# A convolution feeding a gated FFN on one core: four steps of sixteen clip on ScalarE, the convolution's taps are spread over other steps, and the low parts' products come last

## The chip, the cores and the metric

The kernel runs on one core of a Trainium2 chip. The metric is device time in microseconds (us) of one execution. A core has a matmul engine (TensorE, PE in the profile; its weight loads are PEld), two engines for elementwise work that can read the matmul's accumulators in PSUM (VectorE, DVE; ScalarE, ACT), a third that works in SBUF alone (GpSimd, POOL), and SyncE (SP), whose queue issues the DMA transfers here. Each engine takes its instructions strictly in program order and waits where one of them needs something that another engine has not finished.

## The reference

The input x has 8 sequences of 4096 tokens with 192 channels. First comes a causal convolution over 7 tokens whose weights are a softmax per head (8 heads of 24 channels), then a feed-forward layer on the 32768 resulting tokens, 192 to 2048 to 192, with a clipped quadratic between its two matrices:

```python
w = softmax(weight, axis=-1)                       # [8, 7]
out[b, s, h, :] = sum_k w[h, k] * x_pad[b, s + k, h, :]
h = out.reshape(32768, 192) @ w_in                 # [32768, 2048]
g = where(h >= 1, h, where(h <= -1, 0, (h + 1)**2 / 4))
return g @ w_out                                   # [32768, 192]
```

The quadratic can be had in three operations in two ways. The kernel before writes it as max(h, ((c + 1) / 2) squared) with c = h clipped to -1..1. The other form, used by it for the first seven steps only, is max(h, min(1, relu((h + 1) / 2) squared)).

## The kernel before, in words

The tokens are worked in 64 blocks of 512 (the index s, or superblock). Hidden units are taken 256 at a time, so a block takes 8 steps and the program has 512 steps q. Two blocks share one round of convolution work, so everything repeats after 16 steps; i = q mod 16 is the place of a step in this round, and a round has blocks A (i = 0 to 7) and B (i = 8 to 15).

Precision near that of fp32 comes from splitting each operand of a product into a high part, rounded to a shorter format, and a low part, the remainder: `hi` and `lo` (`rh`, `rl` and their swapped copies for the 64 channels above 128, "the rest"), `gh` and `gl` for the hidden values, and weights in two parts. Three partial products are summed for each product.

In step q the program issues, engine by engine:

- PE: `mm1(q)` (line 422), 18 matmuls that form the hidden values `h` of step q in PSUM (two buffers, so `mm1(q)` needs the reads of `h` of step q-2 done), then `mm2(q-2)` (line 462), 20 matmuls that add the product of `gh` and `gl` of step q-2 with the second matrix into four accumulators, `accm` (two) and `accr` (two). In `mm2` eight matmuls on `gh` go into `accm`, then four on `gl` into `accm`, four on `gh` into `accr` and four on `gl` into `accr`. The accumulators have a single buffer: the first `mm2` of the next block (in steps with i = 2 and i = 10) must find them copied out.
- DVE: `act_clip(q)` (line 473, the clip, reading `h` from PSUM), `act_lo(q-1)` (line 497, `gl` = `g` minus `gh`, two operands in SBUF), `act_max(q)` (line 484, reading `h` and `g`), then transposes for the convolution (line 147) and for the output (`osb`, line 534) where such are due.
- ACT: `act_hi(q-1)` (line 491, the cast to `gh`), `act_square(q)` (line 479), in steps with i = 1 and i = 9 the evacuation `evac` of the four accumulators (line 509, four copies to tiles `t`), then what the convolution's plan puts into this step.
- POOL: sums of the evacuated halves (lines 511 and 522), the convolution's adds (line 230) and the low part `lo` (line 252).

The convolution of the next inputs runs beside this on ACT, POOL and DVE. It has three units per round: A and B are the first 128 channels of the two blocks (B is needed in step 8 of the same round, A and R in step 0 of the next), R is the rest of both. A unit begins with a transpose "T" on DVE into a tile `xT`; tap 0 is a scaled copy into `y` on ACT (line 226), each further tap is a product `p` on ACT (line 219) and an add `y + p` on POOL (line 230); at the end "split" makes the high part on ACT (line 248, or 262 for R), the low part on POOL (line 252; for R on DVE, line 263), and the DMAs that swap the two halves of the partitions (lines 235 and 236). `conv_slot(i, ...)` issues the parts that the tables `PLAN_B`, `PLAN_A`, `PLAN_R` name for place i; it stands behind `act_max` in a step. The order on every engine is that in which the program is written; no scheduler moves anything. `xT` and `y` have two buffers each, `p` three.

Of the kernel before, what the change touches and what calls it, by code (L numbers as in the profile page):

```python
# [13 lines left out]
AF = mybir.ActivationFunctionType  # L14
# [16 lines left out]
def lightconv_then_ffn(ctx: ExitStack, tc: tile.TileContext, x, weight, w_in, w_out, out):  # L31
# [24 lines left out]
    nc = tc.nc  # L56
# [8 lines left out]
    NPAIR = NF // 2  # L65
# [44 lines left out]
    def load_unit(c, u, engs=None):  # L110
        ta, tb = 2 * c * TB, (2 * c + 1) * TB
        if u == "rb":
            return load_raw([tb, tb, tb + TB // 2, tb + TB // 2], [P, P + SQ, P, P + SQ], engs,
                            TB // 2)
        if u == "r":
            return load_raw([ta, ta, tb, tb], [P, P + SQ, P, P + SQ], engs)
        return load_raw([ta if u == "a" else tb] * 4, [0, SQ, 2 * SQ, 3 * SQ], engs)
# [14 lines left out]
    NF32 = 2 * NPAIR  # L132
# [257 lines left out]
    NQ = NSB * NPAIR  # L390
    hs, g32, gs, ghs, gls, accs = {}, {}, {}, {}, {}, {}

    def turns(t):

        return t.rearrange("p (o c) -> p c o", o=2)

    def both(t):
        return t.rearrange("p (c o) -> p c o", o=2)
# [4 lines left out]
    def mm1(q):  # L403

        s, j = divmod(q, NPAIR)

        if q == 0:
            h = hs[q] = [ps_o.tile([P, TB], F32, name=n) for n in ("accr1", "accm0")]
        else:
            h = hs[q] = ps_h.tile([P, 2, TB], F32, name="h")  # L410
            h = [h[:, e, :] for e in range(2)]

        if s == 0:
            mms = [(WI[j], us, [xop[s][u] for u in us]) for us in ("ns", "sn", "rr")]
        else:
            mms = [(W[j][:, part], u + u, [xop[s][u, x]] * 2) for u in "nsr"
                   for part, x in ((0, "hi"), (1, "hi"), (0, "lo"))]
        for n, (w, us, x) in enumerate(mms):
            for e in range(2):
                c0 = COL[us[e]][e]  # L420
                to, of = (both(h[e]), turns(x[e][e])) if in_turns(s) else (h[e], x[e][e])
                nc.tensor.matmul(to, w[HALVES[e], c0:c0 + P], of,  # L422
                                 start=(n == 0), stop=(n == len(mms) - 1))

    def new_accs(s):
        accs[s] = {(a, i): ps_o.tile([P, TB], F32, name=f"acc{a}{i}")
                   for a in "mr" for i in range(2)}

    def mm2_first(q):


        s, j = divmod(q, NPAIR)
        g, w = g32.pop(q), WF[j + LAG]
        if j == 0:
            new_accs(s)
        for e in range(2):
            for b in range(TB // P):
                a, c0 = "mr"[b // 2], b % 2 * D
                for i, half in enumerate(HALVES):
                    nc.tensor.matmul(accs[s][a, i][:, c0:c0 + D], g[half, e, b * P:(b + 1) * P],  # L440
                                     w[half, e, :], start=(j == 0 and e == 0 and b % 2 == 0),
                                     stop=(j == NPAIR - 1 and e == 1 and b % 2 == 1))

    def mm2(q):

        s, j = divmod(q, NPAIR)
        gh, gl = ghs.pop(q), gls.pop(q)
        w, wr, k = W[j + LAG], WR[j + LAG], n_in[j + LAG]
        if j == 0:
            new_accs(s)  # L450
        m0, m1, r0, r1, r = ("m", 0, gh), ("m", 1, gh), ("m", 0, gl), ("r", 0, gh), ("r", 0, gl)
        mms = [(e, m) for ms in ((m0, m1), (r0,), (r1,), (r,)) for e in range(2) for m in ms]
        if q == NQ - 1:
            mms = [(0, m) for m in (r1, m0, m1, r, r0)] + [(1, m) for m in (r1, r, m0, m1, r0)]
        first = {a: min(n for n, (e, m) in enumerate(mms) if m[0] == a) for a in "mr"}
        last = {a: max(n for n, (e, m) in enumerate(mms) if m[0] == a) for a in "mr"}
        for n, (e, (a, part, g)) in enumerate(mms):
            c0 = k + e * P
            for i in range(2):
                st = (w[HALVES[i], part, c0:c0 + P] if a == "m"  # L460
                      else wr[HALVES[i], e].rearrange("p a d -> p (a d)"))
                nc.tensor.matmul(both(accs[s][a, i]), st, turns(g[HALVES[i], e, :]),  # L462
                                 start=(j == 0 and n == first[a]),
                                 stop=(j == NPAIR - 1 and n == last[a]))


    def tiles(q):
        return [slice(0, 1), slice(1, 2)] if q == NQ - 1 else [slice(0, 2)]

    def act_clip(q):  # L470
        g = gs[q] = act.tile([P, 2, TB], F32, name="g", bufs=3)
        for e in tiles(q):
            nc.vector.tensor_scalar(out=g[:, e, :], in0=hs[q][:, e, :], scalar1=-1.0, scalar2=1.0,  # L473
                                    op0=ALU.max, op1=ALU.min)

    def act_square(q):
        g = gs[q]
        for e in tiles(q):
            nc.scalar.activation(g[:, e, :], g[:, e, :], AF.Square, bias=0.5, scale=0.5)  # L479

    def act_max(q):
        h, g = hs.pop(q), gs[q]
        for e in tiles(q):
            nc.vector.tensor_tensor(out=g[:, e, :], in0=h[:, e, :], in1=g[:, e, :], op=ALU.max)  # L484
        if q < NF32:
            g32[q] = gs.pop(q)

    def act_hi(q):
        gh = ghs[q] = act.tile([P, 2, TB], F32R, name="gh", bufs=3)
        for e in tiles(q):  # L490
            nc.scalar.copy(gh[:, e, :], gs[q][:, e, :])  # L491
# [209 lines left out]

    PLAN_B = {0: (0, 1), 2: (2, 3), 3: (4, 5), 4: (6,), 5: "split"}
    PLAN_A = {4: ("T", 0), 5: (1, 2), 6: (3, 4), 7: (5, 6), 8: "split"}
    PLAN_R = {7: ("T",), 8: (0, 1, 2), 10: (3, 4), 11: (5, 6), 13: "split"}


    FIRST_B = {2: 2, 3: 3, 4: 4, 5: 5}
# [4 lines left out]
    def conv_slot(i, b, a, r):  # L714
        early = b.c == 0
        plans = ((None if early else b, PLAN_B), (a, FIRST_A if early else PLAN_A),
                 (r, FIRST_R if early else PLAN_R))
        for u, plan in plans:
# [20 lines left out]
    def parts_hi(q):  # L739
        for n, rest in PARTS.get(q, ()):  # L740
            chunks[n].hi(rest)
# [17 lines left out]
    def most(h, g):  # L759

        nc.vector.scalar_tensor_tensor(out=g, in0=g, scalar=1.0, in1=h, op0=ALU.min, op1=ALU.max)
# [75 lines left out]
    for q in range(NQ + DELAY):  # L837
        s, j = divmod(q, NPAIR)
        c, i = divmod(q, 2 * NPAIR)
        done = q - DELAY  # L840
        if q < NQ and i == 0 and c > 0:
            conv_b = conv_n["b"]
        if q < NQ and i == (0 if c > 0 else 4):
            conv_n = {}
            if c + 1 < NB:
                conv_n = {u: Conv(c + 1, u, load_unit(c + 1, u)) for u in "arb"}


        if q == NPAIR:
            mm2_first(done)  # L850
        if q < NQ:
            mm1(q)
        if done >= 0 and q != NPAIR:
            (mm2 if done >= NF32 else mm2_first)(done)

        if q < 2:
            (step_0, step_1)[q]()
        elif q < NPAIR:
            first_step(q)
        else:  # L860
            if q - 1 in gs:
                act_hi(q - 1)
            if q == NPAIR + 1:
                evac(0)
            if q == 2 * NPAIR - 2:
                pending.extend(late)
            if q < NQ:
                let_go()
                act_clip(q)
                act_square(q)  # L870
            if done % NPAIR == NPAIR - 1 and done >= NPAIR:
                (evac if done < NQ - 1 else evac_last)(done // NPAIR)
            parts_hi(q + 1)
            if q - 1 in gs:
                act_lo(q - 1, nc.vector)
            parts_lo(q, (True,))
            if q < NQ:
                let_go()
                act_max(q)
                parts_lo(q, (False,))  # L880
                conv_slot(i, conv_b, conv_n.get("a"), conv_n.get("r"))

            m, r = (DELAY, DELAY + 1) if s > 1 else (NPAIR - 2, NPAIR - 1)
            if q < NQ and j == m:
                evac_rest(s - 1)
                store(s - 1, "m")
            elif q < NQ and j == r:
                store(s - 1, "r")
        if q < NQ and i == 2 * NPAIR - 1 and conv_n:
            conv_n["b"].transpose()  # L890
        if q == NQ - 4:
            plain = ob.tile([P, TB // SQ, SQ], F32, name="osb").rearrange("p j b -> p (j b)")[:, 0:P]
            diagonal(plain, 0)
# [26 lines left out]
```

## Time and profile before

| what | value |
|---|---|
| median of 3 runs | 2170.52 us (2169.75 to 2170.53) |
| the profiled execution, its own time | 2170.33 us |
| its span, first to last instruction | 2168.6 us |
| granted TensorE clock | 0.999 |
| instructions in the span | 48144 |
| PEld busy | 1875.8 us, 86% |
| DMA traffic | 110.83 MB, mean 51 GB/s |

The profile gives, per engine, the busy time and its share of the span; groups of instructions by line and shape with their count, the busy time and the mean duration; and for each engine what ended the times in which it waited. Matmuls overlap one another, so a PE that is 99% busy may still lose time: what tells is the time from the start of one step's `mm1` to that of the next. A timeline row gives the start, the duration, the engine, the line, and in square brackets the idle time before it with the instruction that ended it.

### The profile page before, as it was taken

Reading aid. Unit: us, or ns where it says so; the run is one execution under the profiler, and the core shown is the slowest. Engines: PE = TensorE matmul, PEld = TensorE weight load, DVE = VectorE, ACT = ScalarE, POOL = GpSimd, SP = SyncE. Lnnn points to the kernel's source line nnn. Section 1 sums busy time; section 2 is a strip of 40 time slices with the busy share of each in tenths; the row PEclk is TensorE's granted clock in tenths of the full one; section 3 lists DMA queues with packets and bytes.
Section 4 is the critical chain, followed back from the end, with each engine's and each line's share of the span. In section 5 each row is a group of like instructions: output and inputs, shape, how many; then the busy total and the mean of one; then the engine's idle time right before and its main releaser. Section 6 shows DMA issues by size and latency. Waiting matters only on the chain.

```text
span 2168.6 us, 48144 instructions
## 1 busy us (share of the span) xinstructions
PE 2153.0 (99%) x19646; PEld 1875.8 (86%) x19646; DVE 2084.0 (96%) x1883; ACT 1684.8 (78%) x2153; POOL 1139.4 (53%) x868
## 2 busy tenths in 40 slices
PE   9999999999999999999999999999999999999999
PEld 6998888888888888888888888888888888998887
DVE  8899999999999999999999999999999999999998
ACT  7778877778777788777887787877878777788775
POOL 1556644566445565555654456644556545565451
PEclk9999999999999999999999999999999999999999
DMA  6222222222222222222122222222222222212211
GB/s 165 51 53 42 46 50 51 53 51 42 51 48 50 55 41 53 51 48 55 37 51 51 51 53 48 44 49 48 53 55 40 53 51 47 56 35 53 51 35 25
DMA packets 439197, 110.83 MB, mean 51 GB/s; under 512 B 407360, under 2 KB 414912, under 8 KB 438976
## 3 DMA queue, kind: packets, MB, share of 16 engines
q1 hardware_dynamic: 438816, 107.65, 25.9%
q8 instruction: 155, 2.54, 0.5%
q14 instruction: 66, 0.54, 0.1%
q10 hardware_dynamic: 160, 0.10, 0.0%
HBM read 32.84 MB, written 25.17 MB: 27 GB/s over the span
## 4 chain that ended last, share of the span: by engine, by line
DVE 27%; PE 24%; ACT 19%; POOL 13%; issue 13%; SPq 3%; DMA 1%; POOLq 0%; DVEq 0%; ACTq 0%
POOL y L230 11%; PE h L422 10%; DVE g L484 9%; DVE g L473 8%; PE accm L462 7%; DVE gl L497 7%; ACT g L479 6%; ACT gh L491 5%; PE accr L462 4%; ACT t L509 4%; DVE osb L534 2%; SPq L95 2%; ACT p L219 2%; POOL lo L252 2%; DMA raw<-in_x_dram 1%
## 5 line engine op out<-in xcount | busy, mean ns | idle before, releaser
L230 POOL TENSOR_TENSOR y<-y,p 128x512 f32<-128x512 f32 x546 | 793.8, 1454 | 751.0 <-DVE g L484 541.5
L497 DVE TENSOR_TENSOR gl<-g,gh 128x1024 fp32r<-128x1024 f32 (+1 forms) x497 | 734.4, 1478 | 51.6 <-ACT gh L491 41.3
L491 ACT CAST gh<-g 128x1024 fp32r<-128x1024 f32 (+1 forms) x497 | 520.4, 1047 | 255.4 <-DVE g L484 244.1
L422 PE MATMUL h<-hi,w 64*128 64x512 f32 x4032 | 701.2, 377 | 0.0
L479 ACT ACTIVATE g<-g 128x1024 f32<-128x1024 f32 (+1 forms) x505 | 535.1, 1060 | 167.3 <-DVE g L473 157.0
L484 DVE TENSOR_TENSOR g<-h,g 128x1024 f32<-128x1024 f32 (+1 forms) x505 | 613.3, 1215 | 8.3 <-ACT g L479 4.4
L473 DVE TENSOR_SCALAR g<-h 128x1024 f32<-128x1024 f32 (+1 forms) x505 | 604.7, 1198 | 11.6 <-PE h L422 10.6
L462 PE MATMUL accm<-gh,w 64*128 64x512 f32 x3968 | 604.2, 378 | 9.3 <-ACT t L509 9.1
L422 PEld LDWEIGHTS h<-hi,w 64*128 64x128 f32 x4032 | 523.7, 186 | 47.9
L422 PE MATMUL h<-lo,w 64*128 64x512 f32 x2016 | 540.5, 376 | 0.0
L462 PEld LDWEIGHTS accm<-gh,w 64*128 64x128 f32 x3968 | 449.4, 186 | 77.0 <-ACT t L509 29.4
L462 PE MATMUL accm<-gl,w 64*128 64x512 f32 x1984 | 379.2, 381 | 0.0
L219 ACT ACTIVATE p<-xT,wk 128x512 f32<-128x512 f32 x562 | 376.2, 714 | 0.0
L462 PE MATMUL accr<-gh,wr 64*128 64x512 f32 x1984 | 373.4, 376 | 0.0
L462 PE MATMUL accr<-gl,wr 64*128 64x512 f32 x1984 | 373.4, 376 | 0.0
L422 PEld LDWEIGHTS h<-lo,w 64*128 64x128 f32 x2016 | 330.2, 186 | 24.6
L422 PE MATMUL h<-rh,w 64*128 64x512 f32 x992 | 293.5, 376 | 0.0
L422 PE MATMUL h<-rhi,w 64*128 64x512 f32 x992 | 293.5, 376 | 0.0
L462 PEld LDWEIGHTS accm<-gl,w 64*128 64x128 f32 x1984 | 250.9, 186 | 33.4 <-DVE gl L497 12.3
L462 PEld LDWEIGHTS accr<-gl,wr 64*128 64x128 f32 x1984 | 257.3, 186 | 24.8 <-DVE gl L497 0.2
L462 PEld LDWEIGHTS accr<-gh,wr 64*128 64x128 f32 x1984 | 257.3, 186 | 24.7 <-ACT gh L491 0.2
L422 PEld LDWEIGHTS h<-rhi,w 64*128 64x128 f32 x992 | 184.5, 186 | 14.9
(141 smaller groups left out, 1867.6 us busy)
## 6 DMA issues: line engine op xcount, KB each, us to landing
out_dram<-osb SPq DMA_DIRECT2D x366, 64.0 KB
raw<-in_x_dram SPq DMA_DIRECT2D x334, 68.0 KB
hi<-hi SPq DMA_DIRECT2D x126, 128.0 KB
lo<-lo SPq DMA_DIRECT2D x126, 128.0 KB
rhi<-rh SPq DMA_DIRECT2D x62, 128.0 KB
rlo<-rl SPq DMA_DIRECT2D x62, 128.0 KB
words<-in_moe_w_in_dram SPq DMA_DIRECT2D x16, 192.0 KB
words<-in_moe_w_out_dram SPq DMA_DIRECT2D x8, 384.0 KB
```

Of the source, the lines that this page charges most:

```text
L95: (engs[i] if engs else nc.sync).dma_start(out=raw[i * SQ:(i + 1) * SQ, lo:n // SQ + 1, :], in_=src.rearrange("(j a) b -> a j b", a=SQ),)
L219: nc.scalar.mul(p, self.xT[:, SH + k:SH + k + TB], wk[:, self.wsel, k:k + 1])
L230: nc.gpsimd.tensor_add(y, y, self.product(k))
L252: eng.tensor_sub(lo, self.y, hi.bitcast(F32))
L422: nc.tensor.matmul(to, w[HALVES[e], c0:c0 + P], of, start=(n == 0), stop=(n == len(mms) - 1))
L462: nc.tensor.matmul(both(accs[s][a, i]), st, turns(g[HALVES[i], e, :]), start=(j == 0 and n == first[a]), stop=(j == NPAIR - 1 and n == las ...
L473: nc.vector.tensor_scalar(out=g[:, e, :], in0=hs[q][:, e, :], scalar1=-1.0, scalar2=1.0, op0=ALU.max, op1=ALU.min)
L479: nc.scalar.activation(g[:, e, :], g[:, e, :], AF.Square, bias=0.5, scale=0.5)
L484: nc.vector.tensor_tensor(out=g[:, e, :], in0=h[:, e, :], in1=g[:, e, :], op=ALU.max)
L491: nc.scalar.copy(gh[:, e, :], gs[q][:, e, :])
L497: eng.tensor_sub(gl[:, e, :], g[:, e, :], gh[:, e, :])
L509: nc.scalar.copy(t[i][:, n], acc[a, i][:, n])
```

## The change

Three things are changed.

1. `by_act(q)` is true where i is 0, 4, 5 or 12, from step 16 to step 509. In such a step ACT forms relu(0.5 h + 0.5) from PSUM (line 479 of the new file) in place of DVE's clip, and squares it in place (line 488); `act_max` becomes `most`, one DVE instruction that takes the minimum with 1 and the maximum with `h` (line 775). The relu is issued at the head of ACT's step, in front of the cast of step q-1. In the other steps nothing changes here; their square is line 491 in the new file, the cast 505, the clip 482, `gl` 511, the maximum 498.
2. `mm2` keeps its eight matmuls on `gh` for `accm`, but then takes `accr`'s four on `gh`, and the eight on `gl` come last.
3. The three plans name other places. B: taps 1 to 6 in steps 2, 3 and 4, two each. A: the transpose stays in step 4, tap 0 moves from step 4 to 5, taps to steps 6, 7 (three of them) and 8, the split from step 8 to 10. R: the transpose moves from step 7 to 4, tap 0 alone stays in step 8, the others go two each to steps 10, 11 and 12; the split stays in step 13.

Counted over the program, DVE issues 124 instructions fewer (the clips; 124 maxima become `most`), ACT 124 more; POOL, PE and SP issue as many as before.

```diff
--- before.py
+++ after.py
@@ -449,7 +449,7 @@
         if j == 0:
             new_accs(s)
         m0, m1, r0, r1, r = ("m", 0, gh), ("m", 1, gh), ("m", 0, gl), ("r", 0, gh), ("r", 0, gl)
-        mms = [(e, m) for ms in ((m0, m1), (r0,), (r1,), (r,)) for e in range(2) for m in ms]
+        mms = [(e, m) for ms in ((m0, m1), (r1,), (r0,), (r,)) for e in range(2) for m in ms]
         if q == NQ - 1:
             mms = [(0, m) for m in (r1, m0, m1, r, r0)] + [(1, m) for m in (r1, r, m0, m1, r0)]
         first = {a: min(n for n, (e, m) in enumerate(mms) if m[0] == a) for a in "mr"}
@@ -467,20 +467,34 @@
     def tiles(q):
         return [slice(0, 1), slice(1, 2)] if q == NQ - 1 else [slice(0, 2)]
 
+    BY_ACT = (0, 4, 5, 12)
+
+    def by_act(q):
+
+        return q % (2 * NPAIR) in BY_ACT and NF32 <= q < NQ - 2
+
     def act_clip(q):
         g = gs[q] = act.tile([P, 2, TB], F32, name="g", bufs=3)
+        if by_act(q):
+            nc.scalar.activation(g, hs[q], AF.Relu, bias=0.5, scale=0.5)
+            return
         for e in tiles(q):
             nc.vector.tensor_scalar(out=g[:, e, :], in0=hs[q][:, e, :], scalar1=-1.0, scalar2=1.0,
                                     op0=ALU.max, op1=ALU.min)
 
     def act_square(q):
         g = gs[q]
+        if by_act(q):
+            nc.scalar.activation(g, g, AF.Square)
+            return
         for e in tiles(q):
             nc.scalar.activation(g[:, e, :], g[:, e, :], AF.Square, bias=0.5, scale=0.5)
 
     def act_max(q):
         h, g = hs.pop(q), gs[q]
-        for e in tiles(q):
+        if by_act(q):
+            most(h, g)
+        for e in () if by_act(q) else tiles(q):
             nc.vector.tensor_tensor(out=g[:, e, :], in0=h[:, e, :], in1=g[:, e, :], op=ALU.max)
         if q < NF32:
             g32[q] = gs.pop(q)
@@ -701,9 +715,9 @@
 
 
 
-    PLAN_B = {0: (0, 1), 2: (2, 3), 3: (4, 5), 4: (6,), 5: "split"}
-    PLAN_A = {4: ("T", 0), 5: (1, 2), 6: (3, 4), 7: (5, 6), 8: "split"}
-    PLAN_R = {7: ("T",), 8: (0, 1, 2), 10: (3, 4), 11: (5, 6), 13: "split"}
+    PLAN_B = {0: (0,), 2: (1, 2), 3: (3, 4), 4: (5, 6), 5: "split"}
+    PLAN_A = {4: ("T",), 5: (0,), 6: (1, 2), 7: (3, 4, 5), 8: (6,), 10: "split"}
+    PLAN_R = {4: ("T",), 8: (0,), 10: (1, 2), 11: (3, 4), 12: (5, 6), 13: "split"}
 
 
     FIRST_B = {2: 2, 3: 3, 4: 4, 5: 5}
@@ -858,6 +872,9 @@
         elif q < NPAIR:
             first_step(q)
         else:
+            ahead = q < NQ and by_act(q)
+            if ahead:
+                act_clip(q)
             if q - 1 in gs:
                 act_hi(q - 1)
             if q == NPAIR + 1:
@@ -866,7 +883,8 @@
                 pending.extend(late)
             if q < NQ:
                 let_go()
-                act_clip(q)
+                if not ahead:
+                    act_clip(q)
                 act_square(q)
             if done % NPAIR == NPAIR - 1 and done >= NPAIR:
                 (evac if done < NQ - 1 else evac_last)(done // NPAIR)
```

How this moves instructions is seen at three places. The first is ACT in steps 4 and 5 of a round (from the cast of step 3 to the last convolution piece of step 5). Before:

```order
L491 CAST gh<-g 128x1024
L479 ACTIVATE g<-g 128x1024
L219 ACTIVATE p<-xT,wk 128x512
L226 ACTIVATE y<-xT,wk 128x512
L491 CAST gh<-g 128x1024
L479 ACTIVATE g<-g 128x1024
L248 CAST hi_14329<-y 128x512
L219 ACTIVATE p<-xT,wk 128x512 x2
```

and with the change, from the relu of step 4:

```order
L479 ACTIVATE g<-h 128x1024
L505 CAST gh<-g 128x1024
L488 ACTIVATE g<-g 128x1024
L219 ACTIVATE p<-xT,wk 128x512 x2
L479 ACTIVATE g<-h 128x1024
L505 CAST gh<-g 128x1024
L488 ACTIVATE g<-g 128x1024
L248 CAST hi_14331<-y 128x512
L226 ACTIVATE y<-xT,wk 128x512
```

A's tap 0 (`y<-xT`), which needs the transpose that DVE issues at the end of step 4, stood ahead of the cast `gh` of step 5 and now stands behind it; a relu that reads `h` stands ahead of each cast.

The second is DVE in the same two steps. Before:

```order
L473 TENSOR_SCALAR g<-h 128x1024
L497 TENSOR_TENSOR gl<-g,gh 128x1024
L484 TENSOR_TENSOR g<-h,g 128x1024
L147 STREAM_TRANSPOSE xT<-raw 128x544
L473 TENSOR_SCALAR g<-h 128x1024
L497 TENSOR_TENSOR gl<-g,gh 128x1024
L484 TENSOR_TENSOR g<-h,g 128x1024
```

and with the change:

```order
L511 TENSOR_TENSOR gl<-g,gh 128x1024
L775 SCALAR_TENSOR_TENSOR g<-g,h 128x1024
L147 STREAM_TRANSPOSE xT<-raw 128x544 x2
L511 TENSOR_TENSOR gl<-g,gh 128x1024
L775 SCALAR_TENSOR_TENSOR g<-g,h 128x1024
```

Both clips are gone, and R's transpose, which came in step 7, stands behind A's.

The third is `mm2` on PE, its last twelve matmuls. Before:

```order
L462 MATMUL accm_5826<-gl,w_96 128x512
L462 MATMUL accm_5827<-gl,w_96 128x512
L462 MATMUL accm_5826<-gl,w_96 128x512
L462 MATMUL accm_5827<-gl,w_96 128x512
L462 MATMUL accr_5828<-gh,wr_104 128x512
L462 MATMUL accr_5829<-gh,wr_104 128x512
L462 MATMUL accr_5828<-gh,wr_104 128x512
L462 MATMUL accr_5829<-gh,wr_104 128x512
```

(four on `gl` for `accr` follow) and with the change:

```order
L462 MATMUL accr_5825<-gh,wr_104 128x512
L462 MATMUL accr_5826<-gh,wr_104 128x512
L462 MATMUL accr_5825<-gh,wr_104 128x512
L462 MATMUL accr_5826<-gh,wr_104 128x512
L462 MATMUL accm_5823<-gl,w_96 128x512
L462 MATMUL accm_5824<-gl,w_96 128x512
L462 MATMUL accm_5823<-gl,w_96 128x512
L462 MATMUL accm_5824<-gl,w_96 128x512
```

The first matmul on `gl` comes four matmuls later than it did, the first into `accr` four earlier.

## The prediction, made before the changed kernel ran

> **What bounds the kernel now.** I read the page's busy times first: PE is busy throughout, and DVE nearly so, hence either may set the pace.
>
> ```profile
> PE 2153.0 (99%) x19646; PEld 1875.8 (86%) x19646; DVE 2084.0 (96%) x1883; ACT 1684.8 (78%) x2153; POOL 1139.4 (53%) x868
> ```
>
> What PE could do at best is in the windows view for `mm1`'s line alone (us, then PE and PEld busy with counts). 18 matmuls are one step. The first window begins where a round begins; the second lies in the last round, in which no new A and R are convolved.
>
> ```profile
> 152.65:2091.20 1938.55, 1049.74 (x8352) 859.39 (x8353) 1.00 0.26 49
> 2091.20:2152.70 61.50, 34.73 (x270) 28.29 (x271) 1.00 0.12 23
> ```
>
> The last round does 270/18 = 15 steps in 61.50 us, 4.100 us each. The long stretch has 8352/18 = 464 steps in 1938.55 us, 4.178 each. At 4.100 they would take 1902.4, so 36.1 us are lost over 29 rounds, 1.25 a round. That is all PE can win there. A matmul's share of a full step is 4.100/38 = 0.108 us.
>
> The waits view for 150 to 2100 us (who waited for whom: us, times, longest) says for what:
>
> ```profile
> DVE gl L497 <- ACT gh L491: 39.6, 106, 0.6
> ...
> PEld accm L462 <- ACT t L509: 29.4, 58, 0.7
> PEld accm L462 <- DVE gl L497: 12.3, 54, 0.3
> PE accm L462 <- ACT t L509: 9.1, 28, 0.3
> ```
>
> PE's line waits for two things alone: the evacuation (58 weight loads, two in each of 29 rounds) and `gl`. One round's timeline shows both, in steps 9 and 10:
>
> ```profile
> 1057.60 2.65 POOL L230 TENSOR_TENSOR y<-y,p 128x512 f32<-128x512 f32 x2
> ...
> 1058.54 0.59 PE L422 MATMUL h<-hi,w 64*128 64x512 f32 x4
> ...
> 1059.20 2.13 DVE L497 TENSOR_TENSOR gl<-g,gh 128x1024 fp32r<-128x1024 f32 x1
> ...
> 1060.48 1.03 PE L462 MATMUL accm<-gh,w 64*128 64x512 f32 x8
> ...
> 1061.26 1.21 DVE L484 TENSOR_TENSOR g<-h,g 128x1024 f32<-128x1024 f32 x1
> ...
> 1061.39 0.70 PE L462 MATMUL accm<-gl,w 64*128 64x512 f32 x4
> ...
> 1062.39 1.21 DVE L473 TENSOR_SCALAR g<-h 128x1024 f32<-128x1024 f32 x1
> 1062.43 3.65 POOL L230 TENSOR_TENSOR y<-y,p 128x512 f32<-128x512 f32 x2
> ...
> 1062.79 0.59 PE L422 MATMUL h<-hi,w 64*128 64x512 f32 x4
> ...
> 1063.63 1.06 ACT L479 ACTIVATE g<-g 128x1024 f32<-128x1024 f32 x1
> ...
> 1064.59 1.06 ACT L509 COPY t<-accm 128x512 f32<-128x512 f32 x2
> ...
> 1065.21 1.61 PE L462 MATMUL accm<-gh,w 64*128 64x512 f32 x8 [0.32 <-ACT t L509]
> 1065.54 1.09 ACT L509 COPY t<-accr 128x512 f32<-128x512 f32 x2
> ```
>
> Step 9 starts at 1058.54 and its `mm2` at 1060.48, 1.94 later; so step 10, from 1062.79, wants its accumulators at 1064.73. The first copies begin at 1064.59, and `mm2` starts at 1065.21 and stumbles: 0.85 lost. The copies are late because they stand behind the square (1063.63), which needs the clip (1062.39), which stands behind the maximum (1061.26) and a `gl` that took 2.13 us, with a POOL add running, where one takes 1.22 alone (row 1047.66 below). `h` of step 9 is complete at most 0.38 (one matmul, row below) after 1060.48, at 1060.86: the clip is 1.5 us late because DVE is. Step 9 lost 1062.79 - 1058.54 - 4.10 = 0.15 to that `gl`. The remaining 0.25 of a round lies in step 6:
>
> ```profile
> 1045.20 0.73 DVE L147 STREAM_TRANSPOSE xT<-raw 128x544 f32<-128x544 f32 x1
> ...
> 1045.96 0.73 ACT L226 ACTIVATE y<-xT,wk 128x512 f32<-128x512 f32 x1 [1.32 <-DVE xT L147]
> ...
> 1046.60 1.03 ACT L491 CAST gh<-g 128x1024 fp32r<-128x1024 f32 x1
> ...
> 1047.66 1.22 DVE L497 TENSOR_TENSOR gl<-g,gh 128x1024 fp32r<-128x1024 f32 x1 [0.62 <-ACT gh L491]
> ...
> 1047.95 1.24 PE L462 MATMUL accm<-gh,w 64*128 64x512 f32 x8
> ...
> 1048.93 0.48 PE L462 MATMUL accm<-gl,w 64*128 64x512 f32 x2
> ```
>
> A's tap 0 on ACT waits for its transpose, the cast waits behind it, `gl` for the cast, and PE, due for `gl` at 1047.95 + 8 x 0.108 = 1048.81, for `gl`.
>
> **The change, part by part.** Durations come from the groups by line and shape (count, then busy us, mean ns, idle before):
>
> ```profile
> L497 DVE TENSOR_TENSOR gl<-g,gh 128x1024 fp32r<-128x1024 f32 x495 | 733.2, 1481 | 51.1 <-ACT gh L491 40.8
> ...
> L473 DVE TENSOR_SCALAR g<-h 128x1024 f32<-128x1024 f32 x503 | 603.4, 1200 | 11.2 <-PE h L422 10.1
> ...
> L491 ACT CAST gh<-g 128x1024 fp32r<-128x1024 f32 x495 | 519.2, 1049 | 254.0 <-DVE g L484 242.7 <-PE h L422 4.0
> ...
> L219 ACT ACTIVATE p<-xT,wk 128x512 f32<-128x512 f32 x562 | 376.2, 714 | 0.0
> ...
> L422 PE MATMUL h<-rl,w 64*128 64x512 f32 x496 | 186.5, 376 | 0.0
> ...
> L263 DVE TENSOR_TENSOR rl<-y,rh 128x512 fp32r<-128x512 f32 x31 | 21.1, 681 | 0.6 <-ACT rh L262 0.6
> ...
> L262 ACT CAST rh<-y 128x512 fp32r<-128x512 f32 x31 | 18.7, 603 | 0.7 <-POOL y L129 0.7
> L761 DVE SCALAR_TENSOR_TENSOR g<-g,h 128x1024 f32<-128x1024 f32 x7 | 8.5, 1215 | 0.0
> ...
> L754 ACT ACTIVATE g<-h 128x1024 f32<-128x1024 f32 x7 | 7.1, 1018 | 2.4 <-PE h L422 2.4
> ```
>
> Relu, square and `most` run in this kernel already (line 761 for `most`, 754 for the relu, 1.02 us from PSUM). `most` costs what the maximum does, 1.215 against 1.21 (row 1061.26). So 124 clips of 1.20 leave DVE (149 us: 2084 becomes 1935) and 124 relus of 1.02 come to ACT (126: 1685 becomes 1811, some 85% of the new span). No engine's sum reaches PE's; what counts is the order within a round.
>
> *Clips of steps 4 and 5.* Consecutive DVE rows lie 1.13 apart (1061.26 to 1062.39), so 2.26 us go from in front of step 9's clip, more than its 1.5 of lateness; R's transpose moves from step 7 to 4, also in front, and takes nothing more. From then on DVE needs 3 x 1.13 = 3.4 of a step's 4.10, or 4.3 where POOL blocks `gl` (2.13 against 1.22), so lateness grows by at most 0.2 a step from 6 to 9. Clip 9 then starts at 1060.86 to 1061.4, clip and square take 1.21 + 1.06, and the two `accm` copies end 1.06 later, at 1064.2 to 1064.8 on this round's times; wanted at 1064.73, or 1064.58 without step 9's loss. The gain is 0.6 to 0.85 a round; I take 0.8, since a `gl` blocked in every step is the extreme, which gives 23.2 of 29 x 0.85 = 24.7.
>
> *A's tap 0 behind the cast, the relu in front.* In step 5 (`mm1` from 1047.95 - 1.94 - 4.10 = 1041.91) `h` is complete by 1044.23. Relu 1.02, cast 1.05, `gl` 1.22 (2.13 if blocked) end at 1047.5 to 1048.4. ACT itself may be late by step 4's sum, 1.02 + 1.05 + 1.06 + 2 x 0.71 = 4.55, less 4.10: 0.45 more, to 1048.9. PE now wants `gl` twelve matmuls into `mm2`, at 1047.95 + 1.29 = 1049.24. All 0.25 of step 6 goes, 7.3 us over 29 rounds; below nothing it can't fall on these rows.
>
> *The order in `mm2`.* `gl` is wanted 4 x 0.108 = 0.43 later; step 9's was late by 1061.39 - 1060.48 - 0.86 = 0.05 at its first matmul. Its 0.15 goes: 4.4 us. The price is `accr`, wanted 0.86 instead of 1.29 into `mm2`. Step 10's copies would all end about 2.04 (1064.59 to 1066.63) after they begin, in time if they begin by 1063.4, 0.2 late at 1063.7, which my 0.8 contains. The other evacuation, before step 2, loses nothing today:
>
> ```profile
> 1029.45 1.06 ACT L479 ACTIVATE g<-g 128x1024 f32<-128x1024 f32 x1
> ...
> 1030.42 1.05 ACT L509 COPY t<-accm 128x512 f32<-128x512 f32 x2
> ...
> 1031.36 1.09 ACT L509 COPY t<-accr 128x512 f32<-128x512 f32 x2
> ...
> 1031.55 1.24 PE L462 MATMUL accm<-gh,w 64*128 64x512 f32 x8
> ```
>
> `accr`'s copies end at 1032.45, and it will be wanted at 1031.55 + 0.86 = 1032.41. With relu, cast, square and `most` in step 0 (1.02 + 1.05 + 1.06 + 1.22 = 4.35 after `h`) the next clip starts within 0.2 us of today's. Cost 0 to 0.2 a round; I take 0.05, 1.5 us.
>
> *The moved taps.* Counts on ACT, POOL and SP stay. Step 7 holds three products, 1.05 + 1.06 + 3 x 0.71 = 4.24, 0.14 over a step, with 3.53 in step 6 before it. A's split in step 10 still leaves its swaps 20 us until step 0. Nothing, then, but a bound above from R, the third rival.
>
> *Sum.* 2170.33 (this execution; 0.19 under the median) - 23.2 - 7.3 - 4.4 + 1.5 = 2136.9: **2137 us**.
>
> **The contention rule.** The row: `gl` reads two tiles in SBUF and takes 2.13 beside a POOL add, 1.22 alone, 1.48 on average; clip and maximum, which read `h` from PSUM, take 1.21 in the same stretch. The Trainium skill ("SBUF — State Buffer", Who interferes with whom) says that a VectorE instruction with two SBUF inputs and a GpSimd one that reads SBUF exclude each other for a whole instruction, and that one with a single SBUF input meets no such bar. That speaks against this change as far as it goes: it removes 124 clips, which were never blocked, and none of the 16 `gl` of a round. By that rule the 4.3 us a round of blocking (16 x (1.48 - 1.21)) stay, as in the sum; were all sixteen blocked by 0.9, DVE would need 10 us more a round and no gain would be left, but POOL's 53% makes that remote.
>
> **Rivals.** *The evacuation stays half late* (chance 0.13). Blocked `gl` in steps 7 and 8, or ACT with its 4.55 and 4.24 us steps, holds square 9 back. For it: POOL has three of A's adds there. Against: steps 6 and 8 are short on ACT. With 0.4 a round left, 2137 + 10 = 2147; if step 10 loses as much as now, 2137 + 23 = 2160.
>
> *The gain is given back* (0.05): DVE stays late because its free time is filled by waiting for casts that now stand behind a relu. The cast of step q-1 can't start before `h` of step q is there plus 1.02; today's wait of `gl` for `gh`, 39.6 us in 106 cases, would grow. Against: DVE has 2.26 us less to do in just these steps. Time: 2165 to 2174.
>
> *Slower* (0.08): R's last add. Its taps 5 and 6 move from step 11 to 12 while the split stays in step 13; there DVE's `rl` waits for ACT's `rh`, which waits for POOL's last add, and everything DVE does afterwards waits too. Step 12 on ACT takes 4.55 from `h` at 2.32, so the last product is there 6.9 into step 12, 2.8 into step 13; two adds take 2.65, or 3.65 when blocked, so the last ends 5.5 to 6.5 into step 13, and `rh` (0.60) by 7.1, while DVE is free at 5.7. Behind `rl`, clip, `gl` and maximum end 4.1 later, by 11.2, and must free `h` for step 16 at 12.3. So 1.1 us of room: an add that ends 1.1 + 1.25 = 2.4 us later than I think, after 8.9, costs more than the change gains. At 9.5 it is 1.9 a round: 2134 + 29 x 1.9 = 2189. The longest blocking in the rows is 1.0 us an add, and it would take two more of those.
>
> **How the numbers follow.** The forecast, 2133 to 2142, has 0.74; the first rival 0.13, the second 0.05, the third 0.08. Below all 36.1 us gone, 2134.2, lies only scatter; so the range is 2133 to 2153, which leaves out the end of the first rival, the second and the third, less than 0.2. A difference of 0.2%, 4.3 us, is what can be told from none. Faster: 0.74 + 0.13 + a little of the second = 0.88; the same 0.04; slower 0.08.
>
> **What would show it.** Right: 4.10 us a step over the same 464 steps, no wait of `accm` for `t`, no `y` (226) waiting for `xT`, DVE near 91%. Wrong: in step 10 or 2 a wait of `accm` or `accr` for `t` (the evacuation), in steps 14 to 16 a wait of `h` or `gl` behind `rl` (the third rival), `gl` means above 1.6 us (blocking). The forecast falls if ACT, not DVE, holds the squares back.

## The result, and the profile after

The changed kernel takes 2136.39 us, median of 5 runs (2135.03 to 2136.80), against 2170.31 (2169.75 to 2170.53) before: a ratio of 0.9843 with a 95% interval of 0.9828 to 0.9857. The forecast was 2137, in a range of 2133 to 2153. The profiled execution took 2136.80 us, its span 2135.1.

The page's busy times, and its chain of work that ended last (share of the span by engine):

```profile
PE 2127.2 (100%) x19646; PEld 1965.4 (92%) x19646; DVE 1955.1 (92%) x1759; ACT 1797.2 (84%) x2277; POOL 1151.7 (54%) x868
...
PE 99%; ACT 0%; DVE 0%; issue 0%; DVEq 0%; POOL 0%; POOLq 0%; ACTq 0%
```

DVE has given up 129 us and ACT gained 112. The chain, which before ran over all engines, is now 99% PE. The windows view for `mm1`'s line, the same 464 steps and the same 15 steps at the end as in the prediction:

```profile
153.00:2055.90 1902.90, 1068.87 (x8352) 918.35 (x8353) 1.00 0.27 50
2055.90:2117.40 61.50, 34.73 (x270) 28.29 (x271) 1.00 0.12 23
```

464 steps take 1902.90 us where 1902.4 is the least that PE's 4.100 us a step allow; before they took 1938.55. All 36 us that PE lost in these rounds are back. The rest of the program is about 2 us longer in this profile: its last step begins 17.6 us before the end of the span, against 15.9 before (more on that under the last experiment).

In the waits view for 150 to 2066 us PE has lost its line of waits. What is left is on the other engines:

```profile
DVE gl L511 <- ACT gh L505: 78.3, 135, 1.7
ACT g L491 <- DVE g L482: 74.3, 143, 1.0
...
ACT gh L505 <- DVE g L498: 53.3, 59, 1.6
...
ACT g L479 <- PE h L422: 44.0, 59, 1.6
...
DVE g L482 <- PE h L422: 34.8, 113, 0.5
DVE rl L263 <- ACT rh L262: 20.0, 29, 0.7
...
PEld accr L462 <- ACT t L523: 0.2, 1, 0.2
```

DVE's clip now waits for PE's `h` (34.8 us; 3.5 before in the same rounds): DVE is early where it used to be late. No `y` waits for `xT` any more (38.6 us before). The wait of `rl` for `rh`, the prediction's third rival, is there, 0.7 us in each of 29 rounds, and costs nothing. Steps 9 and 10 of the same round as in the prediction, in the timeline:

```profile
1045.17 1.05 ACT L505 CAST gh<-g 128x1024 fp32r<-128x1024 f32 x1 [0.44 <-DVE g L498]
1045.28 1.23 DVE L482 TENSOR_SCALAR g<-h 128x1024 f32<-128x1024 f32 x1 [0.21 <-PE h L422]
...
1046.54 1.06 ACT L491 ACTIVATE g<-g 128x1024 f32<-128x1024 f32 x1 [0.33 <-DVE g L482]
...
1047.05 0.79 PE L422 MATMUL h<-hi,w 64*128 64x512 f32 x4
...
1047.51 1.06 ACT L523 COPY t<-accm 128x512 f32<-128x512 f32 x2
...
1048.45 1.09 ACT L523 COPY t<-accr 128x512 f32<-128x512 f32 x2
...
1048.99 1.22 PE L462 MATMUL accm<-gh,w 64*128 64x512 f32 x8
```

The clip at 1045.28 is that of step 9 ("clip 9"); it starts as soon as `h` is there. Step 10 starts at 1047.05, the evacuation 0.46 into it (1.80 before), and `mm2` at 1048.99, 1.94 after the step's start, without a wait.

Groups for the same stretch (150 to 2066 us):

```profile
L511 DVE TENSOR_TENSOR gl<-g,gh 128x1024 fp32r<-128x1024 f32 x468 | 693.2, 1481 | 85.0 <-ACT gh L505 78.3
...
L775 DVE SCALAR_TENSOR_TENSOR g<-g,h 128x1024 f32<-128x1024 f32 x117 | 141.7, 1211 | 0.0
...
L479 ACT ACTIVATE g<-h 128x1024 f32<-128x1024 f32 x117 | 119.2, 1019 | 44.0 <-PE h L422 44.0
```

`gl` takes as long as before in the mean (1481 ns); the relu took 1019 ns (1018 in the kernel before), `most` 1211 (1215).

### The profile page after: what moved, and what is told of

It reads as the page before. It is cut to its first block, busy times and chain, and to the rows that moved or that the text cites. A ratio compares the mean times of both kernels' runs of the same rounds, so it can differ in the third digit from the quotient of the medians.

```text
span 2135.1 us, 47827 instructions
## 1 busy us (share of the span) xinstructions
PE 2127.2 (100%) x19646; PEld 1965.4 (92%) x19646; DVE 1955.1 (92%) x1759; ACT 1797.2 (84%) x2277; POOL 1151.7 (54%) x868
## 4 chain that ended last, share of the span: by engine, by line
PE 99%; ACT 0%; DVE 0%; issue 0%; DVEq 0%; POOL 0%; POOLq 0%; ACTq 0%
PE h L422 47%; PE accm L462 30%; PE accr L462 20%; PE accr L440 1%; PE accm L440 1%; PE accr L190 0%; PE accm L623 0%; PE accr L422 0%; PE h L578 0%; PE accm L181 0%; PE accr L578 0%; PE h L155 0%; DVE t L572 0%; PE accr L667 0%; ACT xT L168 0%
## 5 line engine op out<-in xcount | busy, mean ns | idle before, releaser
L422 PEld LDWEIGHTS h<-hi,w 64*128 64x128 f32 x4032 | 576.8, 186 | 30.2
L422 PE MATMUL h<-lo,w 64*128 64x512 f32 x2016 | 581.9, 376 | 0.0
L462 PEld LDWEIGHTS accm<-gh,w 64*128 64x128 f32 x3968 | 483.1, 186 | 30.3
L482 DVE TENSOR_SCALAR g<-h 128x1024 f32<-128x1024 f32 x381 | 461.2, 1211 | 43.3 <-PE h L422 42.9
L491 ACT ACTIVATE g<-g 128x1024 f32<-128x1024 f32 x381 | 402.4, 1056 | 104.4 <-DVE g L482 89.5
L498 DVE TENSOR_TENSOR g<-h,g 128x1024 f32<-128x1024 f32 x381 | 462.5, 1214 | 5.5 <-ACT g L491 3.6
L525 POOL TENSOR_TENSOR sum<-t 128x512 f32<-128x512 f32 (+1 forms) x124 | 155.8, 1280 | 575.6 <-ACT t L523 464.6
L422 PEld LDWEIGHTS h<-lo,w 64*128 64x128 f32 x2016 | 374.8, 186 | 15.6 <-DMA lo<-lo 0.2
L462 PEld LDWEIGHTS accr<-gh,wr 64*128 64x128 f32 x1984 | 284.0, 186 | 15.3 <-ACT t L523 0.2
L462 PEld LDWEIGHTS accm<-gl,w 64*128 64x128 f32 x1984 | 284.1, 186 | 15.1
```

Source lines behind the costliest of these rows:

```text
L422: nc.tensor.matmul(to, w[HALVES[e], c0:c0 + P], of, start=(n == 0), stop=(n == len(mms) - 1))
L525: nc.gpsimd.tensor_add(y[:, n], t[0][:, n], t[1][:, n])
```

## The experiments

All of them were made from the two kernels; every one was timed beside the kernel before on its chip. Besides the time, the profile gives for each step how much longer it took from the start of its `mm1` to that of the next than 4.101 us, the mean where nothing is lost. The table has the mean over the 29 rounds from step 32 to 495 for the places that lose anything; parts 1, 2 and 3 are the clips on ScalarE, the order in `mm2`, and the plans.

```
kernel                     median us   lost per round, us, at i =
                                       2     6     7     9     10    15,0   all
before                     2170.3      0.01  0.23  -     0.14  0.85  -      1.23
part 1 alone               2184.6      -     0.63  -     0.15  0.87  -      1.65
part 2 alone               2172.6      0.01  0.03  0.07  0.07  1.13  -      1.30
part 3 alone               2158.8      0.46  0.22  -     -     0.11  -      0.82
parts 1 and 2              2187.0      -     0.36  0.10  0.13  1.15  -      1.74
parts 2 and 3              2158.6      0.47  0.03  0.08  -     0.22  -      0.81
parts 1 and 3              2134.6      -     -     -     -     -     -      0.00
all (the change)           2136.4      -     -     -     -     -     -      0.00
all, ScalarE in 4, 5 only  2145.9      0.37  -     -     -     -     -      0.37
all, ScalarE in 0, 12 only 2143.0      0.01  0.01  0.05  -     0.23  -      0.29
before, no POOL adds       2134.5      -     -     -     -     -     -      0.00
all, two more POOL adds    2184.8      0.01  -     -     -     -     1.65   1.65
```

(With part 3 alone, steps 13 and 14 lose 0.03 together, with parts 2 and 3 0.02.)

My theory was the prediction's: step 10 is lost because DVE, held up by blocked `gl`, is 1.5 us late; two clips fewer bring it back; the other parts mend steps 6 and 9 by themselves. The rival was that ScalarE's full step 8 makes the evacuation late. How late DVE is in step 9 can be read as the time from the end of `mm1(9)` to the start of its clip: 1.72 us before and 0.04 with the change, each the mean of the 29 rounds.

### Each part alone

The edits, on the kernel before. Part 1:

```diff
+    BY_ACT = (0, 4, 5, 12)
...
+        if by_act(q):
+            nc.scalar.activation(g, hs[q], AF.Relu, bias=0.5, scale=0.5)
+            return
```

> The kernel before with part 1 of the change alone (relu and square on ScalarE in steps 0, 4, 5, 12), old plans and old order of mm2. My theory: the loss of step 10 comes from DVE being 1.5 us late there, and two clips of 1.13 us less take that away; step 9 goes with it; of step 6's 0.25 us a round some may stay, as A's tap 0 still stands ahead of the cast. 2137 to 2146 us, DVE near 92%, step 10 loses under 0.2 us. The rival, that ScalarE's full step 8 (a split, a tap 0 and two products) makes the evacuation late, expects step 10 to lose at least 0.6 us still: 2155 to 2165.

Part 2:

```diff
-        mms = [(e, m) for ms in ((m0, m1), (r0,), (r1,), (r,)) for e in range(2) for m in ms]
+        mms = [(e, m) for ms in ((m0, m1), (r1,), (r0,), (r,)) for e in range(2) for m in ms]
```

> The kernel before with part 2 alone (in mm2 the eight matmuls on gl last). If the terms of the prediction add up, the waits for gl in steps 6 and 9 go and 2159 to 2163 us remain. If instead DVE sets the pace from step 4 to step 10, what is saved in steps 6 and 9 is lost again at the evacuation in step 10, which in addition is wanted 0.43 us earlier for accr: step 10 loses 1.0 to 1.7 us and the time is 2168 to 2185. I hold the second likelier.

Part 3:

```diff
-    PLAN_A = {4: ("T", 0), 5: (1, 2), 6: (3, 4), 7: (5, 6), 8: "split"}
-    PLAN_R = {7: ("T",), 8: (0, 1, 2), 10: (3, 4), 11: (5, 6), 13: "split"}
+    PLAN_A = {4: ("T",), 5: (0,), 6: (1, 2), 7: (3, 4, 5), 8: (6,), 10: "split"}
+    PLAN_R = {4: ("T",), 8: (0,), 10: (1, 2), 11: (3, 4), 12: (5, 6), 13: "split"}
```

(and `PLAN_B` as in the change)

> The kernel before with part 3 alone (the three plans). My theory: the clips are still all on DVE, so DVE stays as full as it was, and the round still loses about 1 us, wherever it shows: 2160 to 2172 us. The rival (ScalarE's step 8 was the cause, and the new plans relieve it): step 10 loses under 0.2 us and the time is 2136 to 2146.

Measured: 2184.59 us (ratio to before 1.0066, 1.0051 to 1.0081) for part 1, 2172.63 (1.0012, 1.0003 to 1.0021) for part 2, 2158.79 (0.9948, 0.9934 to 0.9963) for part 3. Added up, the three differences (+14.5, +2.5 and -11.3) make +5.6 us; together the parts give -33.9.

Part 1 alone makes the kernel *slower*, which neither the theory nor the rival expected. Its timeline in steps 5 and 6 of a round says why:

```profile
1051.12 0.73 DVE L147 STREAM_TRANSPOSE xT<-raw 128x544 f32<-128x544 f32 x1
...
1051.89 0.72 ACT L226 ACTIVATE y<-xT,wk 128x512 f32<-128x512 f32 x1 [1.63 <-DVE xT L147]
...
1052.52 1.00 ACT L479 ACTIVATE g<-h 128x1024 f32<-128x1024 f32 x1
...
1053.42 1.03 ACT L505 CAST gh<-g 128x1024 fp32r<-128x1024 f32 x1
...
1054.48 1.23 DVE L511 TENSOR_TENSOR gl<-g,gh 128x1024 fp32r<-128x1024 f32 x1 [2.63 <-ACT gh L505]
...
1054.50 1.13 PE L462 MATMUL accm<-gh,w 64*128 64x512 f32 x8
```

DVE, without its clips, is done with the transpose earlier, and then stands idle for 2.63 us, since the cast it waits for stands behind a relu, which stands behind A's tap 0, which waited for the transpose. The 2.26 us that left DVE came back as this wait; DVE goes into step 9 as late as before (1.74 us), and step 10 loses 0.87. Step 6 loses more than before, because the cast itself is late for `mm2`. The theory counted the clips rightly and overlooked the wait that takes their place: by these rows, two clips fewer help only if the cast is ready by then.

Part 2 alone did what the second half of its expectation says: steps 6 and 9 lose 0.27 us less, step 10 0.28 more.

Part 3 alone takes most of step 10's loss away (0.85 to 0.11), as the rival said, though its time lies in neither range. ScalarE is not shown to be the reason: DVE is less late in step 9, 0.82 us instead of 1.72. The `gl` of steps 7, 8 and 9 of a round (the last stands behind the clip of step 9) and the evacuation:

```profile
1051.99 1.99 DVE L511 TENSOR_TENSOR gl<-g,gh 128x1024 fp32r<-128x1024 f32 x1
...
1053.85 6.25 POOL L230 TENSOR_TENSOR y<-y,p 128x512 f32<-128x512 f32 x4 [0.95 <-ACT p L219]
...
1056.28 1.30 DVE L511 TENSOR_TENSOR gl<-g,gh 128x1024 fp32r<-128x1024 f32 x1
...
1059.89 1.29 DVE L511 TENSOR_TENSOR gl<-g,gh 128x1024 fp32r<-128x1024 f32 x1
...
1060.85 1.05 ACT L523 COPY t<-accm 128x512 f32<-128x512 f32 x2
```

The long `gl` has moved from step 8, where it took 2.13, to step 7. From the end of the maximum of step 4 to that of step 8, DVE takes 16.19 us instead of 17.19 in the mean of the 29 rounds: its wait for the cast falls from 0.81 to 0.12, and the four `gl` from 6.06 to 5.65. The greater part is thus the wait, and PE shows the gain at step 10. Two moves bear on that wait: tap 0 now stands behind the cast, and R's transpose, 0.7 us of work that came in step 7, fills the time in which DVE waited. No run parts the two.

Step 6, which the prediction meant to mend with tap 0, still loses 0.22. Now two transposes stand in front of step 5's clip, which is 2.34 us late (1.62 before); `gl` waits for no cast and PE waits for `gl` all the same:

```profile
1042.44 1.36 DVE L147 STREAM_TRANSPOSE xT<-raw 128x544 f32<-128x544 f32 x2
...
1043.73 1.19 DVE L482 TENSOR_SCALAR g<-h 128x1024 f32<-128x1024 f32 x1
...
1044.84 1.21 DVE L511 TENSOR_TENSOR gl<-g,gh 128x1024 fp32r<-128x1024 f32 x1
...
1046.10 0.30 PEld L462 LDWEIGHTS accm<-gl,w 64*128 64x128 f32 x4 [0.17 <-DVE gl L511]
```

The evacuation before step 2, which lost nothing, now loses 0.46: R's last taps come a step later, `rl` makes DVE wait 0.69 us in step 13, and DVE is still 0.6 later than before in step 1. No run moved R's taps alone.

### The adds on POOL left out

On the kernel before, the adds of the convolution's taps in all rounds but the first are left out (products are still formed), so `y` stays at tap 0:

```diff
-                    nc.gpsimd.tensor_add(y, y, self.product(k))
+                    self.product(k)
```

> The kernel before without the convolution's adds on POOL after the first round (the products are still formed; y stays at tap 0). This measures what the blocking of gl by POOL's adds is worth. My theory: gl falls from a mean of 1.48 us to about 1.23, DVE is no longer late in step 9, steps 9 and 10 lose under 0.2 us together; step 6, where ScalarE waits for A's transpose, keeps 0.1 to 0.25: 2137 to 2143 us. If ScalarE's queue is the cause, step 10 still loses 0.6 us or more: 2155 to 2168.

Measured: 2134.49 us, no step losing 0.01. The groups and the waits:

```profile
L511 DVE TENSOR_TENSOR gl<-g,gh 128x1024 fp32r<-128x1024 f32 x463 | 591.9, 1278 | 38.4 <-ACT gh L505 33.8
```

```profile
ACT y L226 <- DVE xT L147: 38.6, 29, 1.3
DVE gl L511 <- ACT gh L505: 33.8, 84, 0.7
...
PEld accm L462 <- ACT t L523: 0.2, 1, 0.2
```

With `gl` at 1.28 us instead of 1.48, the order of all other work unchanged, nothing is lost at all, and the clip of step 9 is 0.04 us late. Nothing else got faster that could explain it: every other large group of DVE and ACT keeps its mean within 2%, and in the kernel before neither ACT nor DVE waited for POOL in these rounds, so leaving out the adds freed no queue of theirs. ScalarE's step 8 is as full as it was, which rules the rival out. That settles the cause: DVE's lateness from blocked `gl`. It goes further than the theory: tap 0 on ACT still waits for the transpose (38.6 us, as before) and `gl` for the cast, yet step 6 loses nothing. That wait was not by itself the cause of step 6's loss, as the prediction had it; DVE's lateness made it one.

### Each part undone

From the changed kernel, one part at a time is put back as it was: the order in `mm2`,

```diff
-        mms = [(e, m) for ms in ((m0, m1), (r1,), (r0,), (r,)) for e in range(2) for m in ms]
+        mms = [(e, m) for ms in ((m0, m1), (r0,), (r1,), (r,)) for e in range(2) for m in ms]
```

> The changed kernel with the old order of mm2 (parts 1 and 3). The prediction gave the new order 4.4 us, for step 9, less 1.5 us at step 2: by that the time rises to about 2139. The trace of the changed kernel says otherwise: gl 7 ends 1.8 us before the old order would want it and no step has gl later than 0.6 us before that point, so the order is worth nothing once DVE is not late: 2135 to 2138 us, no step losing 0.05 us.

the plans,

```diff
-    PLAN_A = {4: ("T",), 5: (0,), 6: (1, 2), 7: (3, 4, 5), 8: (6,), 10: "split"}
+    PLAN_A = {4: ("T", 0), 5: (1, 2), 6: (3, 4), 7: (5, 6), 8: "split"}
...
```

> The changed kernel with the old plans (parts 1 and 2). The prediction's terms leave 7.3 us of step 6, less the time that gl is wanted later: 2137 to 2144. What the run of part 1 alone showed (in step 5 DVE waits 2.6 us for a cast that stands behind a relu, which stands behind A's tap 0 and its transpose) says that the clips of steps 4 and 5 then buy nothing and DVE is as late as before in step 9: what is not lost in step 6 is lost in step 10, 1.4 to 1.9 us a round, 2178 to 2192 us. I now hold this one.

and the clips,

```diff
-    BY_ACT = (0, 4, 5, 12)
+    BY_ACT = ()
```

> The changed kernel with every clip on DVE (parts 2 and 3). The prediction's terms put 23.2 us on the clips: 2160. After the run of part 3 alone, which lost 0.46 us in step 2, 0.22 in step 6 and 0.11 in step 10 and was 11 us faster than before, I expect the loss of step 6 to go (gl is wanted 0.43 us later) and step 2 to lose 0.5 to 0.9, since accr is wanted earlier and DVE sets the pace: 2152 to 2163 us, no more than 0.3 in step 10.

Measured: 2134.63 without the new order, 2186.96 without the new plans (1.0076, 1.0061 to 1.0091), 2158.59 without the clips on ScalarE (0.9946, 0.9931 to 0.9961). In the changed kernel the order is worth nothing. The plans are worth 51 us where the other two parts are there and 11 where they aren't; the clips 22 where the plans are there, and they cost 14 where they aren't. Without the plans the waits show the chain that part 1 alone had, one link further: PE now waits for `h` too, as the late cast delays `most`:

```profile
DVE gl L511 <- ACT gh L505: 166.2, 145, 2.6
...
PEld accm L462 <- ACT t L523: 31.8, 58, 0.8
PE accm L462 <- ACT t L523: 11.4, 29, 0.4
PEld h L422 <- DVE g L775: 10.6, 29, 0.4
```

### Two of the four steps at a time

```diff
-    BY_ACT = (0, 4, 5, 12)
+    BY_ACT = (4, 5)
```

> The changed kernel with ScalarE clipping in steps 4 and 5 alone. The prediction's terms need no more than these two: 2137 us. The rival from the run of part 3 alone: steps 12 and 0 are what keeps DVE from being late after R's rl wait (0.7 us in step 13) and so at the evacuation before step 2; without them step 2 loses 0.2 to 0.6 us a round, 2142 to 2155 us, and no other step loses anything.

```diff
-    BY_ACT = (0, 4, 5, 12)
+    BY_ACT = (0, 12)
```

> The changed kernel with ScalarE clipping in steps 0 and 12 alone, the complement of the run with 4 and 5 alone. If the two pairs serve two different places, step 2 loses nothing here and steps 6, 7 and 10 lose what they lost with all clips on DVE, 0.2 to 0.35 us a round: 2140 to 2147 us. If the pair 0 and 12 is enough, because DVE then enters step 2 with less lateness, 2135 to 2138.

Measured: 2145.86 us with 4 and 5, 2143.00 with 0 and 12. The two pairs serve two places. With 4 and 5 alone only step 2 loses, 0.37 us, where the copies are waited for:

```profile
PEld accm L462 <- ACT t L523: 9.2, 31, 0.3
PEld accr L462 <- ACT t L523: 7.1, 29, 0.2
```

With 0 and 12 alone step 2 is clean and steps 7 and 10 lose 0.28. The losses of the two, 0.37 and 0.29, make 0.66 of the 0.81 that a round loses with all clips on DVE.

### The third rival, forced

Two more adds on POOL, of zero onto R's `y`, ahead of its last add, from the third round on:

```diff
+                if self.u == "r" and self.c > 1 and k == K - 1:
+                    for _ in range(2):
+                        nc.gpsimd.tensor_add(yy, yy, zero)
```

> The changed kernel with two more adds on POOL (of zero) before the last add of R in step 12, from the third round on: the third rival of the prediction, forced. Each add takes 1.28 us, so rh and with it rl come 2.6 us later and DVE waits 3.2 us in step 13 instead of 0.7. The prediction gave 1.1 us of room beyond which each round loses, the trace of the changed kernel 1.2 (the maximum of step 14 ends 1.2 us before h is needed): 1.3 to 1.7 us a round over 30 rounds, lost where mm1 waits for h or gl in steps 15 to 0, 2175 to 2190 us, slower than the kernel before. If the wait is hidden after all, under 2150.

Measured: 2184.75 us (1.0065, 1.0050 to 1.0080), slower than before. The waits:

```profile
DVE rl L268 <- ACT rh L267: 95.0, 28, 3.4
...
PEld accm L468 <- DVE gl L517: 25.7, 29, 0.9
...
PE accm L468 <- DVE gl L517: 14.0, 29, 0.5
PEld accm L468 <- ACT gh L511: 12.5, 28, 0.5
...
PE h L428 <- DVE g L504: 6.8, 29, 0.2
```

(The lines of this file are numbered a little higher.) The two adds took 1.71 us each, and the other adds of taps 1.38 in the mean instead of 1.43. DVE waits 3.4 us for `rh` instead of 0.7, 2.7 more, and a round loses 1.65, so 1.05 us of room were used up first. It is lost at the cast, at `gl` and last at `h`, which waits for the maximum of step 14.

### The change against its best variant

The changed kernel again, and the one with the old order of `mm2`, on one chip:

> The changed kernel itself, for the comparison with the next one on the same chip: 2135 to 2137 us. Its first profile ended 2 us later after the last step than those of its variants did; if that is the last output's landing, this profile will have 15.6 us there like the others, and the time will be near 2134.6.

> The changed kernel with the old order of mm2, beside the changed kernel on the same chip. If the new order costs nothing and brings nothing, the two medians agree within 0.5 us and their profiles lose nothing in the steps. If the order matters at the two ends of the program (its first use in step 18, the tail), this one stays 1.5 to 2 us faster.

Measured: 2135.36 us (2134.68 to 2136.41) and 2134.43 (2134.28 to 2134.49); the ratios to before, 0.9838 and 0.9833, have intervals that overlap (0.9824 to 0.9853, 0.9819 to 0.9848). In both profiles the 464 steps lose under 0.1 us, and the last step begins 15.7 us before the end. So the 17.6 of the first profile is not the order's doing in each execution; but the eight executions with the old order lie between 2134.28 and 2134.95 while the nine with the new one spread from 2134.68 to 2136.80. The 2 us lie behind the work: in both profiles of the changed kernel the last output transfer is issued 12.6 us after the last step begins, and the span ends 5.0 us later in one and 3.1 in the other. Nor are they always inside the span: one execution of 2136.51 us has a span of 2132.9. The medians here differ by 0.9 us in favour of the old order; why the new one spreads more is open.

## Why the prediction was right, and where it was wrong

*What bounds the kernel* was right to a fraction of a microsecond: PE's 4.100 us a step and 36.1 us to win. The forecast was right because the change wins all of it. What PE could win was a ceiling, and the terms were slices of that ceiling, so their sum could hardly miss once all losses went. That it came within 0.6 us is partly luck: the steps gave 35.7 us where the sum had 33.4, and the rest of the program took about 2 us more in the profile.

*The cause* (DVE 1.5 us late in step 9 through blocked `gl`) was right, and is shown: without POOL's adds nothing is lost.

*The terms* were wrong as separate sums. The step that failed is the one that gives each loss its own remedy and adds them: 23.2 for the clips of steps 4 and 5, 7.3 for tap 0, 4.4 for the order in `mm2`. In one chain of work on DVE a loss removed at one place comes back at the next:

- "Clips of steps 4 and 5": together with those of 0 and 12, but without the new plans, they made the kernel 14 us slower; in the changed kernel 4 and 5 are worth 7.6 (2143.0 to 2135.4, same chip). Steps 12 and 0, to which the prediction gave nothing, are worth about 10 (2145.9): without them DVE comes late into step 2, by the rows after R's moved taps. All four are worth 22 there, near the 23.2 by chance: 0.47 of the 0.81 us a round is lost at step 2, which the term doesn't contain.
- "A's tap 0 behind the cast": 7.3 foreseen, at step 6. With part 3 alone, tap 0 moved, step 6 loses what it lost before (0.22 and 0.23). In the changed kernel the move is, by the rows, what lets the clips pay: the run of part 1 alone shows the cast behind relu and tap 0, and undoing the plans, of which this is one move, costs 51 us. No run moved tap 0 alone.
- "The order in `mm2`": a net 2.9 foreseen, nothing measured. With DVE on time `gl` is early, and with DVE late the saving moves to step 10.
- "The moved taps ... Nothing, then": the moves also put the long `gl` into another step and R's `rl` behind a wait. Part 3 alone, tap 0 included, is worth 11 us; what the moved taps alone are worth was not measured.

*The engines' sums* were off as well, without harm to the forecast: DVE gave up 129 us where 149 were foreseen and ACT took 112 for 126. The prediction multiplied durations by counts, while rows on one engine overlap (1.21 us long and 1.13 from start to start on DVE), which accounts for about half of the 20 us missing there.

*The rivals.* The second, the gain given back by waiting for casts behind a relu, got 0.05 and is what part 1 does with the old plans. It didn't come with the new ones. The third was sized well: the prediction has `rh` ready by 7.1 us into step 13, the maximum of step 14 ended by 11.2, and 1.1 us of room; in the changed kernel `rh` is ready at 6.8, that maximum ends at 11.1, and the forced run used up 1.05 before it lost anything. The evacuation rival had nothing for it here: the evacuation starts 0.46 us into step 10, inside the 0.35 to 0.95 that follows from the prediction's times for the end of its first two copies (1064.2 to 1064.8, with step 10 at 1062.79 and 1.06 for the two).

*The contention rule* held as weighed: `gl` kept its mean (1484 ns to 1481 in the middle of the program) with a quarter of the clips gone. The page "SBUF — State Buffer" of the Trainium skill (Who interferes with whom) lets a two-input VectorE instruction and a GpSimd one that reads SBUF exclude each other. The run without the adds agrees, with 1278 ns for `gl`; it shows that the whole loss of 36 us hung on this.

## What to carry to other kernels

Where one in-order engine is late through a round, the losses on the critical engine are one loss that shows at several places: take its ceiling (here 464 steps at 4.100 us) as the gain, and don't add up remedies by place. Work taken from the late engine helps only if its next instruction can start: look at what it will wait for then, and at everything queued ahead of that on the other engine. And moving the adds on POOL moves the subtractions on DVE that they hold up (here from step 8 to step 7): ask which ones they will meet.

## What the runs showed of the hardware that was not expected

Sixteen `gl` a round that take 1.48 instead of 1.28 us, 3.2 us in 66.8 on an engine that isn't the bound by its sum, are enough for the whole loss of 36 us: with them it is there, without them it is gone. The change removes the same loss with `gl` as slow as before. And executions of a program whose steps lose nothing can still differ by 2 us at the end: the last step began 17.6 us before the end of the span in one profile of the changed kernel and 15.7 in another, with the last output transfers issued alike.
